# Sparse attention and a Mish layer: three products in other PSUM buffers, and three re-orderings

## The chip, the cores and the metric

The kernel runs on one core of a Trainium2 chip. The metric is the device time of one execution in microseconds (us), as the median of several runs. Five engines work side by side and meet through semaphores: TensorE (PE, with its weight loads shown as PEld), VectorE (DVE), ScalarE (ACT), GpSimd (POOL), and SyncE (SP), which here only issues transfers. Matmul results go to PSUM, which TensorE writes and VectorE and ScalarE read.

## The reference, cut to what matters

Attention over 8 batches of 8 heads, 576 positions, 64 values each. Half of the heads see the 32 positions up to their own ("local", `l`), half those with the same position modulo 32 ("strided", `s`). Then comes a layer of two matrices with a Mish between.

```python
rel = pos[:, None] - pos[None, :]
mask_local = (rel >= 0) & (rel < stride)                 # stride = 32
mask_strided = (rel >= 0) & (pos[None, :] % stride == pos[:, None] % stride)
scores = np.where(masks, scale * q @ k.T, -1e9)
attn = exp(scores - max); attn = attn / sum(attn)
x = (attn @ v), heads side by side                        # 4608 tokens x 512
h = x @ w_in                                              # 512 -> 2048
out = (h * np.tanh(softplus(h))) @ w_out                  # 2048 -> 512
```

## The kernel before

The 4608 tokens are worked off in nine blocks of 512 (`t`), each with a product with `w_in` (`mlp1`), a Mish on ScalarE and a product with `w_out` (`mlp2`). Between the pieces of those products stand the steps of the attention of a later batch: in block `t` that of batch `t + 1`. The first batch stands alone at the head of the program, before the first block.

PSUM has eight banks. Six form three accumulators of two banks (`acc`), two are single buffers that are used in turn (`tile_t`):

```python
def acc(i, name):
    return ps_a.tile([128, 2, 512], F32, tag=f"acc{i}", name=name)

def tile_t(name):
    return ps_t.tile([128, 512], F32, tag="pt", name=name)      # pool with bufs=2
```

Transposes (`t_step_loc0` for q and k, `xt` for the attention's result) and the products with v share the two single buffers. A product with v, `pv`, computes four heads' parts and, in column D, the sum of the weights; VectorE then takes the reciprocal and multiplies, which empties the buffer:

```python
def pv(self, kind, i):
    po = tile_t("po")[:, 0:4 * (D + 1)].rearrange("p (h d) -> p h d", h=4)
    m = WQ if kind == "l" else PN
    self.pv_mm(kind, i, po)
    ...
    nc.vector.reciprocal(rden[0:m, :], po[0:m, :, D])
    nc.vector.tensor_tensor(out=dst..., in0=po[0:m, :, 0:D], in1=rden..., op=ALU.mult)
```

`pv2` does two of them at once in an accumulator (first batch only). `qk(parts, i_acc)` computes scores into an accumulator, from which ScalarE writes the exponentials to SBUF; `mask` multiplies them by a mask on VectorE. The kind "n" is the strided scores of the next batch but with another division into parts.

The steps of batches 2 and 3 (blocks 1 and 2); the list's place i is run after the i-th of 16 pieces of `mlp2`. `x, y, z` are the accumulators. Pieces 0 to 7 sum in z, 8 to 15 in y, and ScalarE copies an accumulator out after its last piece:

```python
Q = lambda i_acc, *parts: (lambda: a.qk(parts, i_acc))
M = lambda kd, i: (lambda: a.mask(kd, i, nc.vector))
V = lambda kd, i: (lambda: a.pv(kd, i))
X = lambda kd, hf: (lambda: a.xt(kd, hf))
...
    [V("s", 4), M(*l0)],                  # 6
    [Q(x, l1), V("s", 5)],                # 7
    [V("s", 6), V("l", 5)],               # 8
    [V("s", 7), M(*l1)],                  # 9
    [V("l", 0), V("l", 1)],               # 10
    [X("s", 0), V("l", 2)],               # 11
    [X("s", 1), V("l", 3)],               # 12
    [V("l", 4), X("l", 0)],               # 13
    [X("l", 1)], [],                      # 14, 15
if z is not None:                         # block 2 only: scores of batch 4
    r[12].append(Q(x, ("n", 0)))
    r[13].append(Q(z, ("n", 1)))
    r[15] += [Q(x, ("n", 2)), M("n", 0), M("n", 1), M("n", 2)]
```

The steps of batch 1 (block 0), where `ts[4]` and `ts[6]` are transposes of k (copied out by VectorE), `ts[5]` and `ts[7]` of q (copied by ScalarE). In this block `mlp2` sums in x and z, and y serves for scores:

```python
    [V("s", 1), M("s", 1), Q(y, ("s", 2))],       # 4
    [V("s", 2), ts[4]],                           # 5
    [V("s", 3), M("s", 2), ts[6], ts[5]],         # 6
    [V("s", 4), ts[7]],                           # 7
    [V("s", 5), Q(y, ("l", 0))],                  # 8
    ...
    [V("l", 3), V("l", 5)],                       # 13
    [V("l", 4), X("l", 0)],                       # 14
    [X("l", 1)],                                  # 15
```

The first batch. `fill` and `fill_acc` are matmuls whose results nobody reads, put where TensorE would otherwise pause:

```python
for i in range(3):
    a.qk([("s", i)], i)                            # scores of s, exponentials
fill(tile_t("fill"), 3)
a.pv2("s", 0, 0)
t_step_loc0(kl0, kTl[:, 0, 32:32 + S], 0, Sc)      # local k, from its transfer lq<-in_k
t_step_loc0(kl0, kTl[:, 1, 32:32 + S], 1, Sc)
a.pv2("s", 2, 1)
a.pv2("s", 4, 2)
fill_acc(0, 2)
t_step_loc0(ql0, qTl[:, 0, :], 0, Sc)              # local q
t_step_loc0(ql0, qTl[:, 1, :], 1, Sc)
a.pv2("s", 6, 0)
for i in range(2):
    a.bias("l", i, i + 1)                          # the mask as a matmul
for i in range(2):
    a.qk([("l", i)], i + 1)
for hp in range(2):
    rows_v_loc01(0, hp, Dv)                        # rows of v, VectorE
...
a.xt("s", 0, Dv)
a.xt("s", 1)
fill_acc(0, 2)
a.pv2("l", 0, 1)
a.bias("l", 2, 0)
a.qk([("l", 2)], 0)
a.pv2("l", 2, 2)
gT, g1 = mlp1(0, accs)                             # accs = (1, 2, 0)
g1.pop(0)()                                        # first large product
```

Of the kernel before, what the change touches and what calls it, by code (L numbers as in the profile page):

```python
# [40 lines left out]
def kernel(ctx, tc, q, k, v, moe_w_in, moe_w_out, out):  # L41
    nc = tc.nc
    B, H, S, D = q.shape
# [29 lines left out]
    qTl = const.tile([128, 2, S], BF16, name="qTl")  # L73
# [16 lines left out]
# [5 lines that stand above are left out]
        return ps_t.tile([128, 512], F32, tag="pt", name=name)  # L95
# [49 lines left out]
    def copy_v_str01(b, eng, j0, j1):  # L145
        cast(
            eng, vs[b % 2][0:PN, :, j0:j1, 0:D],
            vsd[b % 2].rearrange("p (h j d) -> p h j d", h=4, j=CS)[:, :, j0:j1, :],
        )
# [27 lines left out]
    def cast(eng, out_, in_):  # L177
        if eng is nc.scalar:
            nc.scalar.copy(out_, in_)  # L179
        else:  # L180
            eng.tensor_copy(out_, in_)  # L181
# [15 lines left out]
    def str_by_dma(b):  # L197
        for src, dst in ((ks, kTs), (qs, qTs)):
            nc.sync.dma_start_transpose(
                sT(dst, b)[:, 0:16 * SU].rearrange("c (u n) -> c u n", u=16),  # L200
                src[b % 2][0:SU].rearrange("p h x -> p (h x)"),
            )
# [45 lines left out]
    def t_step_loc0(src, dst, hp, eng):  # L248

        tr = tile_t("tr")[:].bitcast(BF16)  # L250
        for j in range(CL):
            for e in range(2):
                nc.tensor.transpose(  # L253
                    tr[64 * e:64 * e + 64, PL * j:PL * j + PL], src[0:PL, 2 * hp + e, j, :],
                    ident[0:PL, 0:PL],
                )
        cast(
            eng, dst.rearrange("c (p j) -> c p j", j=CL),
            tr[:, 0:S].rearrange("c (j p) -> c p j", j=CL),
        )  # L260
# [26 lines left out]
    class Attn:  # L287
# [85 lines left out]
                        start=True, stop=True,  # L373
                    )

        def pv(self, kind, i):
            po = tile_t("po")[:, 0:4 * (D + 1)].rearrange("p (h d) -> p h d", h=4)
            m = WQ if kind == "l" else PN
            self.pv_mm(kind, i, po)
            dst = (x_l if kind == "l" else x_s)[0:m, i, :]  # L380
            rden = small.tile([128, 4], F32, tag="rden", name="rden")
            nc.vector.reciprocal(rden[0:m, :], po[0:m, :, D])  # L382
            nc.vector.tensor_tensor(  # L383
                out=dst.rearrange("p (h d) -> p h d", h=4), in0=po[0:m, :, 0:D],
                in1=rden[0:m, :].unsqueeze(2).to_broadcast([m, 4, D]), op=ALU.mult,
            )
# [95 lines left out]
            [], [], [], [], [], [], [],  # L482
        ]

    def attn_steps(b, x, y, z=None):

        a = Attn(b)
        Q = lambda i_acc, *parts: (lambda: a.qk(parts, i_acc))
# [3 lines that stand above are left out]
        s0, s1, sl2, l0, l1 = ("s", 0), ("s", 1), (("s", 2), ("l", 2)), ("l", 0), ("l", 1)  # L492
        r = [
            [],
            [Q(x, s0), Q(y, s1), M(*s0), M(*s1)],
            [],
            [V("s", 0), V("s", 1)],
            [Q(x, *sl2), Q(y, l0), V("s", 2)],
            [V("s", 3), M("s", 2), M("l", 2)],
            [V("s", 4), M(*l0)],  # L500
            [Q(x, l1), V("s", 5)],
            [V("s", 6), V("l", 5)],
            [V("s", 7), M(*l1)],
            [V("l", 0), V("l", 1)],
            [X("s", 0), V("l", 2)],
            [X("s", 1), V("l", 3)],
            [V("l", 4), X("l", 0)],
            [X("l", 1)], [],
        ]
        if z is not None:  # L510
            r[12].append(Q(x, ("n", 0)))
            r[13].append(Q(z, ("n", 1)))
            r[15] += [Q(x, ("n", 2)), M("n", 0), M("n", 1), M("n", 2)]
        return r


    def attn_steps1(y, ts):

        a = Attn(1)
# [4 lines that stand above are left out]
        return [  # L524
            [lambda: nc.scalar.preload_act_table(AF.Exp)],
            [Q(y, ("s", 0)), lambda: copy_v_str01(1, nc.vector, 0, CS)],
            [M("s", 0), Q(y, ("s", 1))],
            [V("s", 0)],
            [V("s", 1), M("s", 1), Q(y, ("s", 2))],
            [V("s", 2), ts[4]],  # L530
            [V("s", 3), M("s", 2), ts[6], ts[5]],
            [V("s", 4), ts[7]],
            [V("s", 5), Q(y, ("l", 0))],
            [V("s", 6), M("l", 0), Q(y, ("l", 1))],
            [V("s", 7), V("l", 0), M("l", 1), Q(y, ("l", 2))],
            [X("s", 0), V("l", 1), M("l", 2)],
            [X("s", 1), V("l", 2)],
            [V("l", 3), V("l", 5)],
            [V("l", 4), X("l", 0)],
            [X("l", 1)],  # L540
        ]


    def fill(t, n, w=512):

        for _ in range(n):
            nc.tensor.matmul(
                t[:, 0:w], lhsT=kTs[1][:, 512:640], rhs=kTs[1][:, 0:w], start=True, stop=True
            )
# [86 lines left out]
    with tc.manual_schedule():  # L636
        Po, Dv, Sc = nc.gpsimd, nc.vector, nc.scalar
# [4 lines left out]
        kl0, ql0 = [lq0[:, 1536 * i:1536 * i + 1536].rearrange("p (h x) -> p h x", h=4) for i in range(2)]  # L642
# [7 lines left out]
        kl0, ql0 = [x.rearrange("p h (j d) -> p h j d", d=D) for x in (kl0, ql0)]  # L650
# [26 lines left out]
        a = Attn(0)  # L677
# [12 lines left out]
            a.qk([("s", i)], i)  # L690
        fill(tile_t("fill"), 3)
        a.pv2("s", 0, 0)
        t_step_loc0(kl0, kTl[:, 0, 32:32 + S], 0, Sc)
        t_step_loc0(kl0, kTl[:, 1, 32:32 + S], 1, Sc)
        a.pv2("s", 2, 1)
        a.pv2("s", 4, 2)
        fill_acc(0, 2)
        t_step_loc0(ql0, qTl[:, 0, :], 0, Sc)
        t_step_loc0(ql0, qTl[:, 1, :], 1, Sc)
        a.pv2("s", 6, 0)  # L700
        for i in range(2):
            a.bias("l", i, i + 1)
# [44 lines left out]
        for t in range(NBLK):  # L747
            x, y, z = accs
            if t > 0:
                gT, g1 = mlp1(t, accs)  # L750
            at, a1 = [], []
            if t == 0:
                ts = t_steps1()
                at = attn_steps1(y, ts)
                at[1].append(next_loads)
                at[10] += [lambda: str_by_dma(2), lambda: loc_by_dma(2)]
                out_accs, accs = (z, x), (y, z, x)
            else:
                if t <= 2:
                    at = attn_steps(t + 1, x, y, z if t == 2 else None)  # L760
                elif t + 1 < B:
                    a1 = str_steps(t + 1)
                    at = loc_steps(t + 1, x, y)
                if t == 1:
                    at[9].append(lambda: str_by_dma(3))
                if t == 2:
                    Dv.memset(x_s[64:96], 0.0)
                if t + 2 < B:
                    at[9].append(lambda: loc_by_dma(t + 2))
                if 1 < t < B - 3:  # L770
                    at[9].append(lambda: str_by_dma(t + 3))
                out_accs, accs = (z, y), (z, x, y)
            for i, g in enumerate(g1):
                g()
                if i < len(a1):
                    for s in a1[i]:
                        s()
                if t == 0 and i > 7:
                    for n in ((0, 2), (1, 3))[i - 8]:
                        ts[n]()  # L780
            if t > 0 and t + 2 < B:
                cast_qk_loc(t + 2, Po, Po)
                if 1 < t < B - 3:
                    load_qk_str(t + 3)
                if t < 3:
                    cast_v(t + 2, Po, Po)
                else:
                    at[5].append(lambda: cast_v(t + 2, Po, Po))
            if t == 1:
                load_qk_str(4)  # L790
            if t == NBLK - 1:
                mlp2_last(t, gT, (z, y, x))
                break
            for i, g in enumerate(mlp2(t, gT, out_accs, fc_major=(t == 0))):
                g()
                if i < len(at):
                    for s in at[i]:
                        s()
            if t + 3 < B:
                load_qk_loc(t + 3)  # L800
                if t == 1:
                    str_by_dma(4)
                load_v(t + 3)
# [30 lines left out]
```

The softmax here doesn't subtract the row's maximum and nothing guards it: scores larger than these inputs give would overflow.

## Time and profile before

| | |
|---|---|
| Time, median of 3 runs | 306.92 us (305.93 to 307.51) |
| Span of the profiled execution | 305.2 us |
| TensorE busy | 298.5 us, 98% |
| ScalarE, VectorE, GpSimd busy | 59%, 51%, 34% |
| Granted TensorE clock | full in all slices of the page |

How to read it: the span runs from the first instruction to the last. An engine's line names the source line, the operation, output and input, and how often. In brackets stands the idle time before an instruction and what ended it. The chain follows the work back from the last instruction to what released each step, so that it says which engine set the end at each moment. Names with L and a number are lines of the kernel: L366 is the product with v, L382 and L383 its reciprocal and multiply, L253 the transposes of local q and k, L410 and L420 those of the result, L324 the scores, L338 their exponential, L346 the masks on VectorE, L575 `mlp1`, L599 `mlp2`, L606 the copy of its result. Matmuls overlap and their ends are modelled.

### The profile page before, as it was taken

The page shows a single profiled execution, that of the slowest core. Times are in us where ns is not written, and L with a number is a line of the kernel's source. Part 1 is how long each engine was busy: PE and PEld are TensorE (multiplying, and loading weights), DVE is VectorE, ACT ScalarE, POOL GpSimd, SP SyncE. Part 2 cuts the span into 40 slices and gives each one's busy share as a digit, 9 for nine tenths or more (in the row PEclk, how much of TensorE's full clock was granted, in tenths as well). Part 3 has the DMA queues.
Part 4 walks back from the last instruction along what each step waited for, and adds up shares of the span by engine and source line. Part 5 has one row for each costly group of instructions (what it writes and reads, how often), then busy time and mean ns, then how long its engine had stood idle before and what let it go on. Part 6 is the DMA issues. An engine that isn't in the chain of part 4 may idle for free.

```text
span 305.2 us, 6124 instructions
## 1 busy us (share of the span) xinstructions
PE 298.5 (98%) x2552; PEld 160.0 (52%) x2552; DVE 155.8 (51%) x375; ACT 181.3 (59%) x193; POOL 104.1 (34%) x119
## 2 busy tenths in 40 slices
PE   8999999999999999999999999999999999999995
PEld 7664555544554455444579654445444544444444
DVE  4382366202840077489877888788878850000000
ACT  2676625776456764757965786678668746216501
POOL 8662339930470232405940296029500000000000
PEclk9999999999999999999999999999999999999999
DMA  7999999999999999999769995997520120011011
GB/s 138 169 207 193 206 182 140 157 113 257 181 217 124 227 176 193 165 210 176 107 144 178 190 171 144 169 192 121 128 89 0 54 86 0 2 69 69 0 71 69
DMA packets 97552, 41.83 MB, mean 137 GB/s; under 512 B 79605, under 2 KB 91461, under 8 KB 97525
## 3 DMA queue, kind: packets, MB, share of 16 engines
q1 hardware_dynamic: 71708, 28.84, 52.5%
q0 software_dynamic: 25504, 12.31, 32.9%
q8 instruction: 20, 0.33, 0.4%
q10 hardware_dynamic: 312, 0.28, 0.3%
q14 instruction: 8, 0.06, 0.1%
HBM read 36.82 MB, written 9.44 MB: 152 GB/s over the span
## 4 chain that ended last, share of the span: by engine, by line
PE 91%; DVE 3%; DMA 2%; POOL 1%; issue 1%; ACT 1%; ACTq 0%; POOLq 0%
PE psh L575 41%; PE pso L599 35%; PE po L366 5%; PE pso L626 5%; PE ps L324 3%; DMA lq<-in_k_dram 2%; DVE x_l L383 1%; PE tr L253 1%; PE trx L410 1%; DVE x_s L383 1%; PE trx L420 1%; DVE rden L382 0%; ACT Ps L338 0%; POOL qs L110 0%; POOL vs L110 0%
## 5 line engine op out<-in xcount | busy, mean ns | idle before, releaser
L575 PE MATMUL psh<-xT,w_in 128*128 128x512 bf16 (+3 forms) x648 | 130.6, 355 | 0.6 <-DVE rden L396 0.3
L599 PE MATMUL pso<-w_out,gT 128*128 128x512 bf16 x512 | 121.7, 379 | 0.0
L581 ACT ACTIVATE gT<-psh 128x1024 bf16<-128x1024 f32 x72 | 72.4, 1023 | 46.1 <-PE psh L575 46.1
L575 PEld LDWEIGHTS <-w_in 128*128 128x128 bf16 x648 | 60.8, 98 | 55.1 <-issue 0.9
L599 PEld LDWEIGHTS <-gT 128*128 128x128 bf16 x512 | 45.5, 98 | 46.1
L445 DVE STREAM_TRANSPOSE xs_t<-x_s 32x512 bf16<-32x512 bf16 x48 | 33.7, 702 | 0.9
L606 ACT COPY osb<-pso 128x1024 f32<-128x1024 f32 x16 | 17.6, 1100 | 24.8 <-PE pso L599 14.4
L382 DVE RECIPROCAL rden<-po 72x4 f32<-72x4 f32 (+1 forms) x98 | 17.3, 177 | 28.5 <-PE po L366 28.4
L181 POOL CAST kl<-kl 96x768 bf16<-96x768 f32 x10 | 8.4, 870 | 65.5 <-DMA kl<-in_k_dram 65.5
L346 DVE TENSOR_TENSOR Ps<-Ps,consts_sb 72x864 bf16<-72x864 bf16 (+3 forms) x12 | 7.4, 616 | 40.0 <-ACT Ps L338 40.0
L436 DVE STREAM_TRANSPOSE xT<-x_l 32x384 bf16<-32x384 bf16 x48 | 27.3, 569 | 0.7
L181 DVE COPY osb<-pso 128x512 f32<-128x512 f32 (+1 forms) x2 | 1.1, 558 | 51.3 <-PE pso L626 51.3
L383 DVE TENSOR_TENSOR x_s<-po,rden 72x256 bf16<-72x256 f32 x56 | 23.5, 420 | 1.9
L338 ACT ACTIVATE Ps<-ps 72x864 bf16<-72x864 f32 (+3 forms) x21 | 17.4, 860 | 11.1 <-PE ps L324 11.1
L366 PEld LDWEIGHTS <-Ps 72*128 72x128 bf16 x256 | 15.6, 97 | 11.4 <-DVE Ps L346 0.8
L452 ACT COPY xT<-xs_t 128x576 bf16<-128x576 bf16 x8 | 21.4, 2938 | 0.0
L338 ACT ACTIVATE Pl<-ps 128x960 bf16<-128x960 f32 (+1 forms) x20 | 17.2, 877 | 2.6 <-PE ps L324 2.5
L383 DVE TENSOR_TENSOR x_l<-po,rden 96x256 bf16<-96x256 f32 x42 | 17.7, 420 | 1.4
L366 PE MATMUL po<-vs,Ps 72*128 72x65 bf16 (+1 forms) x256 | 18.1, 194 | 0.0
L181 POOL CAST vl<-vl 128x768 bf16<-128x768 f32 (+2 forms) x20 | 15.6, 779 | 6.1 <-DMA vl<-in_v_dram 5.2
L179 ACT COPY xT<-trx 128x576 bf16<-128x576 bf16 x15 | 9.6, 639 | 12.5 <-PE trx L420 9.6
L346 POOL TENSOR_TENSOR Ps<-Ps,consts_sb 72x1008 bf16<-72x1008 bf16 (+1 forms) x9 | 14.5, 1636 | 0.8 <-DVE x_l L383 0.7
(93 smaller groups left out, 242.9 us busy)
## 6 DMA issues: line engine op xcount, KB each, us to landing
out_dram<-osb SPq DMA_DIRECT2D x16, 512.0 KB, 3.9
kl<-in_k_dram SPq DMA_DIRECT2D x5, 576.0 KB, 7.0
ql<-in_q_dram SPq DMA_DIRECT2D x5, 576.0 KB, 10.6
vs<-in_v_dram SPq DMA_DIRECT2D x5, 576.0 KB
vl<-in_v_dram SPq DMA_DIRECT2D x5, 576.0 KB, 9.6
w_out<-in_moe_w_out_dram POOLq DMA_DIRECT2D x4, 512.0 KB, 14.9
ks<-in_k_dram POOLq DMA_DIRECT2D x7, 288.0 KB, 9.8
qs<-in_q_dram POOLq DMA_DIRECT2D x7, 288.0 KB, 10.0
```

Of the source, the lines that this page charges most:

```text
L181: eng.tensor_copy(out_, in_)
L338: nc.scalar.activation(pt[0:n, :, 0:nw], t[0:n, :, o0:o0 + nw], AF.Exp, scale=scale)
L346: meng.tensor_tensor(out=pm, in0=pm, in1=mk[0:n, :].unsqueeze(1).unsqueeze(1).to_broadcast([n, 2, nu, w]), op=ALU.mult,)
L366: nc.tensor.matmul(po[:, h, 0:rhs.shape[-1]], lhsT=pt[0:n, c0:c0 + 128], rhs=rhs, start=True, stop=True,)
L383: nc.vector.tensor_tensor(out=dst.rearrange("p (h d) -> p h d", h=4), in0=po[0:m, :, 0:D], in1=rden[0:m, :].unsqueeze(2).to_broadcast([m, ...
L436: nc.vector.transpose(dst[32 * q:32 * q + 32, :, :, m:m + 32], src[m:m + 32, :, :, q, :])
L445: nc.vector.transpose(xs_t[32 * q:32 * q + 32, :, :, m:m + 32], src[m:m + 32, :, :, q, :])
L452: nc.scalar.copy(xT[:, 2 + c, t0:t0 + S].rearrange("p (n j) -> p j n", j=CS), xs_t[:, :, c, 0:PN])
L575: nc.tensor.matmul(ps[:, u, o:o + n], lhsT=w_in[:, cc, fc * 128:(fc + 1) * 128], rhs=xT[:, cc, a:a + n], start=(cc == 2 and o == 0), stop= ...
L581: nc.scalar.activation(gT[:, 2 * g:2 * g + 2, :], ps[:], AF.Mish)
L599: nc.tensor.matmul(p[:, ot % 2, :], lhsT=gT[:, fc, 128 * ot:128 * ot + 128], rhs=w_out[:, fc, :], start=(fc == 0), stop=(fc == 15),)
L606: nc.scalar.copy(osb[:], p[:])
```

## The change

Six places. One product of batch 1 (`s` 3) moves from a single buffer to accumulator y, and there the mask of part 2 moves behind the two transposes. A second product of batch 1 (`l` 4) moves to y. The product `l` 5 of batches 2 and 3 moves to z. These are meant to leave the two single buffers to the neighbours. The last scores of batch 4, and the masks of the parts before, move one step ahead, so that their exponential is issued ahead of the copy of the last `mlp2` result. In the first batch the second pair of strided products moves ahead of the transposes of local k, to stand where TensorE would wait for k's transfer, and the copy of half of q moves from ScalarE to VectorE.

```diff
-        def pv(self, kind, i):
-            po = tile_t("po")[:, 0:4 * (D + 1)].rearrange("p (h d) -> p h d", h=4)
+        def pv(self, kind, i, i_acc=None):
+            po = tile_t("po") if i_acc is None else acc(i_acc, "po")[:, 0, :]
+            po = po[:, 0:4 * (D + 1)].rearrange("p (h d) -> p h d", h=4)
...
     def attn_steps(b, x, y, z, more):
...
-            [V("s", 6), V("l", 5)],
+            [V("s", 6), lambda: a.pv("l", 5, z)],
...
-        if z is not None:
+        if more:
             r[12].append(Q(x, ("n", 0)))
             r[13].append(Q(z, ("n", 1)))
-            r[15] += [Q(x, ("n", 2)), M("n", 0), M("n", 1), M("n", 2)]
+            r[14] += [Q(x, ("n", 2)), M("n", 0), M("n", 1)]
+            r[15].append(M("n", 2))
...
-            [V("s", 3), M("s", 2), ts[6], ts[5]],
+            [lambda: a.pv("s", 3, y), ts[6], ts[5], M("s", 2)],
...
-            [V("l", 4), X("l", 0)],
+            [lambda: a.pv("l", 4, y), X("l", 0)],
...
         a.pv2("s", 0, 0)
+        a.pv2("s", 2, 1)
         t_step_loc0(kl0, kTl[:, 0, 32:32 + S], 0, Sc)
         t_step_loc0(kl0, kTl[:, 1, 32:32 + S], 1, Sc)
-        a.pv2("s", 2, 1)
         a.pv2("s", 4, 2)
         fill_acc(0, 2)
         t_step_loc0(ql0, qTl[:, 0, :], 0, Sc)
-        t_step_loc0(ql0, qTl[:, 1, :], 1, Sc)
+        t_step_loc0(ql0, qTl[:, 1, :], 1, Dv)
...
-                    at = attn_steps(t + 1, x, y, z if t == 2 else None)
+                    at = attn_steps(t + 1, x, y, z, t == 2)
```

More of the change, by code (lines that the diff above doesn't have):

```diff
@@ L483, in loc_steps, with attn_steps @@
         ]
-    def attn_steps(b, x, y, z=None):
+    def attn_steps(b, x, y, z, more):
         a = Attn(b)
```

## The prediction

> **What bounds the kernel now.** I read the page first: the busy table, then the chain that ended last.
>
> ```profile
> PE 298.5 (98%) x2552; PEld 160.0 (52%) x2552; DVE 155.8 (51%) x375; ACT 181.3 (59%) x193; POOL 104.1 (34%) x119
> ...
> PE 91%; DVE 3%; DMA 2%; POOL 1%; issue 1%; ACT 1%; ACTq 0%; POOLq 0%
> ```
>
> TensorE carries 91% of the chain and nothing in this change removes work from it. So the change can win only what lies between TensorE's instructions: about 9% of 305 us is the outer limit, much of it the start. Next I listed the waits of TensorE and then read the timeline and the chain in order of time at the places that the diff names. A wait's own figure counts from the modelled end of the matmul before it, and matmuls overlap, so I measure holes from start to start, with these lengths from the chain: a 128x512 matmul 0.216 us (0.86 for four), the four products of one `pv` 0.13, twelve 96-row transposes 0.32 (0.63 for 24).
>
> Batch 1, step 6, the chain in order of time:
>
> ```profile
> 43.51 0.19 DVE rden L382
> ...
> 43.72 0.43 DVE x_s L383
> 44.15 0.14 issue
> 44.29 0.45 PE tr L253 x12
> ```
>
> The transposes of q (L253, at 44.29) want the buffer in which the product s3 stood, and wait for VectorE's reciprocal and multiply. The k transposes before them began at 43.40 and hold 0.32, so the hole is 43.72 to 44.29, **0.57 us**.
>
> Batch 1, step 14, TensorE's timeline:
>
> ```profile
> 54.98 0.29 PE L366 MATMUL po<-vl,Pl 128*128 128x65 bf16 x4
> 55.42 0.43 PE L410 MATMUL trx<-consts_sb,x_l 96*128 96x96 bf16 x6 [0.16 <-DVE x_l L383]
> ```
>
> l4 holds 0.13, so the transposes could begin at 55.11. They begin at 55.42: **0.31 us**, for the buffer of l5.
>
> Batch 2, step 8, the whole timeline (the second VectorE line is the one that counts below):
>
> ```profile
> 79.71 1.01 ACT L606 COPY osb<-pso 128x1024 f32<-128x1024 f32 x1 [1.44 <-issue]
> ...
> 80.88 0.28 PE L366 MATMUL po<-vs,Ps 72*128 72x65 bf16 x4
> 80.97 0.42 DVE L383 TENSOR_TENSOR x_s<-po,rden 72x256 bf16<-72x256 f32 x1
> ...
> 81.49 0.29 PE L366 MATMUL po<-vl,Pl 128*128 128x65 bf16 x4 [0.33 <-PE po L366]
> ...
> 82.81 0.18 DVE L382 RECIPROCAL rden<-po 72x4 f32<-72x4 f32 x1 [0.33 <-PE po L366]
> ```
>
> s6 is through at 81.01, l5 starts at 81.49: a hole of 0.48. The wait is named after a TensorE instruction, which had long been done; what ends just before is VectorE's multiply of s5 (81.39), whose buffer l5 takes. In batch 3 the same step shows no hole: s6 at 113.85 and l5 at 113.97.
>
> The end of that stage, where batch 4's last scores stand:
>
> ```profile
> 123.35 1.01 ACT L606 COPY osb<-pso 128x1024 f32<-128x1024 f32 x1 [0.23 <-PE pso L599]
> 123.41 1.04 PE L575 MATMUL psh<-xT,w_in 128*128 128x512 bf16 x4
> 124.26 0.41 ACT L338 ACTIVATE Ps<-ps 72x288 bf16<-72x288 f32 x1
> ...
> 124.71 0.38 PE L575 MATMUL psh<-xT,w_in 128*128 128x512 bf16 x1 [0.26 <-ACT Ps L338]
> ```
>
> The second group of the next product wants the accumulator of those scores; their exponential stands behind the output copy on ScalarE. 123.41 + 0.86 = 124.27, so the hole is **0.44 us**.
>
> The first batch, the chain:
>
> ```profile
> 4.56 7.49 DMA lq<-in_k_dram
> 12.05 0.04 issue
> 12.09 0.70 PE tr L253 x24
> ...
> 13.75 0.45 PE fill L547 x2
> 14.21 0.63 PE tr L253 x24
> ```
>
> TensorE ends s0 and s1 at about 11.5 and idles until local k has landed at 12.05.
>
> **What the Trainium skill says.** "Perfetto Trace Analysis", Identifying the Most-Contended Engine, holds matmul busy time to be a poor measure of how near TensorE is to its limit; the trace agrees, 98% busy with holes of 0.3 to 0.6 us. The same page, Optimization Strategy, has repeated bubbles on the engine that should be full stand for too few buffers; three of the four holes above are that, each ending with the VectorE instruction that frees a buffer. "PSUM — Partial Sum Buffer", PSUM bank collisions raise a hardware error, asks that engines are kept apart by bank, so a product put into accumulator z must await the output copy that reads z: the end at 80.72 is to be checked, not only VectorE. "TensorE: Matmul & The Clock Gate", Step-by-step, has weight loads pulled ahead only where row groups don't conflict; the trace shows something that fits: scores start at 123.24, 0.10 us after the product before has passed (122.28 + 0.86).
>
> **The change, part by part.** No instruction is added or removed.
>
> (1) s3 of batch 1 in accumulator y, with the two transposes ahead of the mask. y was last read by an exponential that ended at 41.51, so s3 doesn't wait. k then takes the buffer of s2 (free at 42.67), q that of the k transposes before (copied by 43.33): no wait. 24 transposes from 43.40 take 0.63, and 0.07 to the next product, as now: 44.10 in place of 44.67, **0.57**. The mask (0.66) moves behind the copy of k (0.74) on VectorE and ends near 45.5, so s4's multiply ends near 46.2; its buffer is next wanted near 46.4. It is close but does not bind. I take 0.55.
>
> (2) l4 of batch 1 in y: the transposes take l3's buffer, free at 54.82. **0.31**. The transposes of the other half start at about 56.25, after l4's multiply (55.94).
>
> (3) l5 in z. For batch 2, z's output copy ends at 80.72, before 81.01, so l5 starts 0.48 earlier. Not all of it stays: VectorE is without a pause until it has multiplied l5 at 82.48, and its chain of s7, mask, l0 and l1 leads to the next product at 85.16, which waits for it. That chain starts at 82.81 after 0.33 of idle; 0.02 of that is needed between instructions. **0.31**. In batch 3: 0, with the copy ending at 113.69 against 113.97.
>
> (4) Batch 4's last scores: their exponential now comes ahead of the output copy (about 123.0 to 123.45), their accumulator is free before 124.27. **0.44**. The output copy slides to about 124.6; its accumulator is wanted by the third group, after 125.1.
>
> (5) The first batch. The exponential for s2 and s3 ends at 11.78 (two take 1.66 from 10.12). s2 and s3 can then run from 11.85 to 12.29 (two such pairs take 0.87, 12.72 to 13.59), add 0.10 to switch, k transposes 12.39 to 13.02, s4 and s5 to 13.46, two fills to 13.89, switch, q transposes at 13.99 in place of 14.13: 0.14 on TensorE, not 0.43, as k has landed meanwhile. Local q landed about 13.6 (issued 5.60, 8.0 to landing), so that doesn't bind. But the half of q now on VectorE (0.74, the size of the kTl copies) is put ahead of the reciprocal of s6, and VectorE is on the path: s6's multiply now ends at 16.35, then come the v rows, a copy of x, and the reciprocal of l0 at 18.08, which releases the first large product at 19.15. With q's copy from about 14.8 to 15.55, s6's multiply would end near 16.4. ScalarE is freed, but TensorE's 0.83 us of bias matmuls cover its copies (end 15.80) already. I take **0.05**.
>
> Sum: 0.55 + 0.31 + 0.31 + 0.44 + 0.05 = 1.66. From 306.92: **305.3 us**. Behind 125 us TensorE runs from product to product (0.86 and 0.13 in turn), so I see nothing that takes the gain back.
>
> **Rivals.** *A new wait on an accumulator.* In batch 3 l5 trails the output copy by only 0.28; for z to be late in both batches would cost about 0.3 each. For it: ScalarE has the copy, exponentials and more in one row. Against: no change ahead of them. That would make it 305.6 to 305.9. *VectorE becomes the bound* in the first batch and in step 7 of batch 1: the first part would lose some 0.2, the second keep only half: 305.8. *Timed by transfers*: if the early part waited for weights, the early gains vanish. Against it, the first large products wait for no transfer in the list of TensorE's waits. *All holes close and VectorE follows*: the first batch gives its 0.3 as well and batch 2 0.41: 304.9.
>
> **Range and chances.** The parts are independent; 0.3 us of uncertainty for the first batch and 0.2 for each of the others make about 0.5. The three runs before spread over 1.6 us, so a median can be off by 0.5 too. Range 304.3 to 306.4. Two per cent is 6.1 us, more than all holes here together: faster 0.01, same 0.98, slower 0.01.
>
> **What would show it.** In the changed trace: q's transposes right behind k's at about 43.7; the transposes after l4 with no wait on VectorE; l5 0.13 after s6 in batch 2; the first group pair of the stage at 123 without a wait for an exponential; the list of TensorE's waits nearly empty; the first large product at 19.1, not 18.8. I would be wrong if l5 is seen waiting for an output copy, if step 7 of batch 1 waits for VectorE, or if the first large product comes later than 19.15.

## The result, and the profile after

The changed kernel takes 304.99 us in the median of 6 runs (304.85 to 305.34), the kernel before 306.55 us in 6 runs (305.93 to 308.07). The ratio is 0.9943, with a 95% interval of 0.9917 to 0.9969. It is faster by about half a per cent, as forecast (305.3).

From the page of the changed kernel, the busy table and the chain that ended last:

```profile
PE 297.8 (98%) x2552; PEld 159.4 (53%) x2552; DVE 155.8 (51%) x376; ACT 180.9 (60%) x192; POOL 103.6 (34%) x119
...
PE 95%; DVE 3%; ACT 1%; issue 0%; ACTq 0%
```

The busy times are as before: TensorE does the same work in a shorter span. Its share of the chain has risen from 91% to 95%, and the transfer of k has left the chain.

From the list of TensorE's waits of the changed kernel (who waited for whom: us in total, times, longest):

```profile
PE fill L549 <- DVE kTs L653: 1.3, 1, 1.3
PE psh L577 <- DVE rden L397: 0.3, 1, 0.3
PE po L366 <- ACT Ps L338: 0.2, 1, 0.2
```

Seven waits have become three, and the last of them is new: in the first batch the product s2 now waits for an exponential.

TensorE's order is fixed, so the span can be cut at its own instructions and each stretch compared. All times in us, from the two profiled executions:

| Stretch, on TensorE | before | after | gain |
|---|---|---|---|
| Start to the first exponential (ScalarE) | 10.12 | 10.02 | 0.10 |
| to the first large product | 9.02 | 8.84 | 0.18 |
| to the first `w_out` product of block 0 | 15.68 | 15.68 | 0 |
| `w_out` products of block 0, with batch 1 | 21.98 | 21.02 | 0.96 |
| `w_out` products of block 1, with batch 2 | 19.16 | 18.67 | 0.49 |
| `w_out` products of block 2, with batch 3 | 19.82 | 19.82 | 0 |
| from there to batch 4's first product with v | 2.16 | 1.73 | 0.43 |

The `w_in` products between take 13.8 in both, and what follows 179.67 in both. The gains add up to 2.17 before rounding, which is what the two spans differ by. Between the medians it is only 1.56: the profiled execution of before, 307.01 us, lies above that kernel's median, and the one of after, 304.85, a little below its own. The experiments tell which of these gains are always there.

The four places in block 0 to 2, in the changed kernel. The chain, batch 1, step 6 (start, length, what):

```profile
43.18 0.63 PE tr L253 x24
43.81 0.97 PE pso L601 x4
```

k's and q's transposes are now one piece of 24. Before, they were two of 12 with a reciprocal and a multiply of VectorE between. TensorE's timeline, batch 1, step 14:

```profile
54.05 0.29 PE L366 MATMUL po<-vl,Pl 128*128 128x65 bf16 x4
54.18 0.42 PE L411 MATMUL trx<-consts_sb,x_l 96*128 96x96 bf16 x6
```

The transposes begin 0.13 after l4, without a wait. The timeline of batch 2, step 8:

```profile
78.46 1.01 ACT L608 COPY osb<-pso 128x1024 f32<-128x1024 f32 x1 [1.44 <-issue]
...
79.63 0.28 PE L366 MATMUL po<-vs,Ps 72*128 72x65 bf16 x4
79.75 0.29 PE L366 MATMUL po<-vl,Pl 128*128 128x65 bf16 x4
```

l5 comes 0.12 after s6; the output copy that empties z ended at 79.47, 0.28 ahead of it. The timeline at the end of block 2:

```profile
121.27 0.41 ACT L338 ACTIVATE Ps<-ps 72x288 bf16<-72x288 f32 x1
121.68 1.89 PE L577 MATMUL psh<-xT,w_in 128*128 128x512 bf16 x8
121.88 1.01 ACT L608 COPY osb<-pso 128x1024 f32<-128x1024 f32 x1 [0.20 <-PE pso L601]
```

The exponential of batch 4's last scores now stands ahead of the output copy, and the first two groups of `mlp1` run as one piece of eight.

### The profile page after: what moved, and what is told of

The parts are those of the page before. It is cut to its first block, busy times and chain, and to the rows that moved or that the text cites. A ratio compares the mean times of both kernels' runs of the same rounds, so it can differ in the third digit from the quotient of the medians.

```text
span 303.1 us, 6121 instructions
## 1 busy us (share of the span) xinstructions
PE 297.8 (98%) x2552; PEld 159.4 (53%) x2552; DVE 155.8 (51%) x376; ACT 180.9 (60%) x192; POOL 103.6 (34%) x119
## 4 chain that ended last, share of the span: by engine, by line
PE 95%; DVE 3%; ACT 1%; issue 0%; ACTq 0%
PE psh L577 41%; PE pso L601 35%; PE po L366 5%; PE pso L628 5%; PE ps L324 3%; PE fill L549 2%; PE tr L253 1%; ACT Ps L338 1%; DVE x_l L384 1%; PE tr L237 1%; PE trx L411 1%; PE ps L297 1%; DVE x_s L384 1%; PE trx L421 1%; DVE rden L383 0%; DVE Pl L346 0%
```

## The experiments

The theory from the traces was that each hole is an affair of its own and closes for good when its cause is taken away. For batch 2 there was a rival. In the kernel before, VectorE's mask of the strided part 2 had taken 1.01 us, while GpSimd was casting k. Timeline of the kernel before:

```profile
78.24 2.10 POOL L181 CAST kl<-kl 96x768 bf16<-96x768 f32 x2 [10.10 <-DMA kl<-in_k_dram]
...
78.37 1.01 DVE L346 TENSOR_TENSOR Ps<-Ps,consts_sb 72x576 bf16<-72x576 bf16 x1
```

In batch 3 the same mask took 0.45, with no cast beside it, and there was no hole either.

### Each part of blocks 0 to 2 left out alone

The medians alone can't tell one part from another: with the exception of s3's, the ratios below have intervals that overlap the changed kernel's 0.9917 to 0.9969. So what a part is worth is read from the stretches, of one profiled execution each.

**l5 back in a single buffer** (batches 2 and 3):

```diff
-            [V("s", 6), lambda: a.pv("l", 5, z)],
+            [V("s", 6), V("l", 5)],
```

> The changed kernel with l5 of batches 2 and 3 back in a single buffer. Theory A (the hole of batch 2 comes from there being two single buffers): l5 waits again 0.4 to 0.5 us after s6 in batch 2, and the time is 0.3 to 0.5 above the changed kernel, 305.3 to 305.5. Theory B (the hole came because the mask of the strided part 2 took 1.01 us instead of 0.45 in that execution, beside GpSimd's cast of k, and made VectorE late): no wait where that mask takes 0.45, in batch 3 never, and a time within 0.15 of the changed kernel's 305.0.

Measured: 305.39 us, ratio to the kernel before 0.9955 (0.9937 to 0.9973). In the profiled execution l5 didn't wait in either batch; the mask of part 2 took 0.45 in both. The timeline of batch 2:

```profile
79.67 0.28 PE L366 MATMUL po<-vs,Ps 72*128 72x65 bf16 x4
79.79 0.30 PE L366 MATMUL po<-vl,Pl 128*128 128x65 bf16 x4
```

So the hole isn't made by the number of buffers alone, as theory A had it. The stretches were still about 0.28 longer each than in the changed kernel (18.95 and 20.10), and the median is what theory A expected. But the loss is elsewhere: in batch 2 the mask of the local part 1 took 0.92 in place of 0.65, beside GpSimd's cast of q, and in batch 3 a mask of part 0 took 0.88 in place of 0.60. It isn't the buffer's either: with l5 in z, the run with batch 4's scores put back (below) has stretches of 18.97 and 20.07, with 0.94 and 0.86 for the same two masks.

**s3 back in a single buffer, with its mask ahead:**

```diff
-            [lambda: a.pv("s", 3, y), ts[6], ts[5], M("s", 2)],
+            [V("s", 3), M("s", 2), ts[6], ts[5]],
```

> The changed kernel with s3 of batch 1 back in a single buffer and its mask back ahead of the transposes. Sum of holes: q's transposes wait again for s3's multiply, 0.57 to 0.64 us between k's transposes and the next product, time 305.6. Rival (VectorE is behind anyway and takes the gain back later in block 0): under 0.3, time 305.0 to 305.3.

Measured: 305.83 us, ratio 0.998 (0.997 to 0.999). Block 0's stretch is 21.81, 0.79 above the changed kernel's. The hole is back, as TensorE's list of waits has it:

```profile
PE tr L253 <- DVE x_s L384: 0.4, 1, 0.4
```

From k's transposes to q's it is 0.89 against 0.28, which is 0.61 of the 0.79; the rest came a step later, behind a mask that took 0.92 beside GpSimd's copy of rows of v.

**l4 back in a single buffer:**

```diff
-            [lambda: a.pv("l", 4, y), X("l", 0)],
+            [V("l", 4), X("l", 0)],
```

> The changed kernel with l4 of batch 1 back in a single buffer. Sum of holes: 0.31 us ahead of the transposes after l4, time 305.3. Rival (the next block waits for ScalarE's output copy, so the start of the product after it doesn't move): no difference, 305.0.

Measured: 305.34 us, ratio 0.9952 (0.9928 to 0.9976); block 0's stretch 21.35, 0.33 above the changed kernel's. The hole stands at the same place, and the next block starts later by as much.

**Batch 4's last scores back in step 15:**

```diff
-            r[14] += [Q(x, ("n", 2)), M("n", 0), M("n", 1)]
-            r[15].append(M("n", 2))
+            r[15] += [Q(x, ("n", 2)), M("n", 0), M("n", 1), M("n", 2)]
```

> The changed kernel with batch 4's last scores and masks back in step 15. Sum of holes: 0.44 us ahead of the second group of the next product, which waits for the exponential, time 305.4. Rival (the third group or the activation behind it takes the gain back): under 0.2, 305.0 to 305.2.

Measured: 305.40 us, ratio 0.9961 (0.9948 to 0.9975). The way to batch 4's first product is 2.16 again, as before the change, and TensorE's list has the wait back:

```profile
PE psh L576 <- ACT Ps L338: 0.3, 1, 0.3
```

**s3 in y, but the mask ahead of the transposes:**

```diff
-            [lambda: a.pv("s", 3, y), ts[6], ts[5], M("s", 2)],
+            [lambda: a.pv("s", 3, y), M("s", 2), ts[6], ts[5]],
```

> The changed kernel with s3 in accumulator y but its mask ahead of the transposes again. If the buffer alone closes the hole: q's transposes follow k's at once; the mask (0.45 to 0.66) then stands ahead of VectorE's copy of k, whose buffer s4 wants, so s4 would wait some 0.4 to 0.6: time 305.4. If the order of the mask doesn't matter: 305.0.

Measured: 305.18 us, ratio 0.9966 (0.9955 to 0.9978); block 0's stretch 21.64, 0.62 above the changed kernel's. In this execution the whole gain of the buffer is gone. The timeline shows where to:

```profile
43.59 0.42 PE L253 MATMUL tr<-consts_sb,ql 96*64 96x96 bf16 x12
...
43.97 0.96 DVE L346 TENSOR_TENSOR Ps<-Ps,consts_sb 72x576 bf16<-72x576 bf16 x1
...
44.85 0.74 DVE L181 COPY kTl<-tr 128x576 bf16<-128x576 bf16 x1
...
45.65 0.45 PE L253 MATMUL tr<-consts_sb,ql 96*64 96x96 bf16 x12 [0.55 <-DVE kTl L181]
```

q's first transposes (43.59) come at once, but VectorE does the mask ahead of its copy of k, so the buffer of k comes free late and the next transposes wait for it. The hole has moved one step on. But the mask was a slow one, 0.96 in place of 0.45, beside GpSimd's copy of rows of v. With 0.45 the copy of k would end 0.51 sooner, and about 0.1 of the 0.62 would be left (an estimate). The medians lie between: on the same chip the kernel that differs from the changed one in the copy of q alone ("the new order alone", below) took 304.94, 0.24 less than this one, which is within the spread of either's runs. So the order can matter, and how much depends on the mask.

### The first batch

**Both edits of the first batch undone:**

```diff
-        a.pv2("s", 2, 1)
         t_step_loc0(kl0, kTl[:, 0, 32:32 + S], 0, Sc)
         t_step_loc0(kl0, kTl[:, 1, 32:32 + S], 1, Sc)
+        a.pv2("s", 2, 1)
...
-        t_step_loc0(ql0, qTl[:, 1, :], 1, Dv)
+        t_step_loc0(ql0, qTl[:, 1, :], 1, Sc)
```

> The changed kernel with both edits of the first batch undone: s2 and s3 behind k's transposes, both halves of q copied by ScalarE. From the two traces the head gained 0.19 (first exponential to first large product 9.03 before, 8.84 after): 305.2. The prediction's 0.05 would give 305.05, and 9.03 to 8.98 for the stretch.

**The new order alone** (q's copy back on ScalarE), and **the split of q alone** (the order back), each by one half of that diff:

> The changed kernel with q's second half back on ScalarE, the early s2 and s3 kept. If the order alone makes the gain (TensorE's bias matmuls cover ScalarE's copies): stretch from the first exponential to the first large product 8.84 or below, as VectorE is also spared 0.76 us: 305.0 or 304.9. If the split of q is needed: the scores of l wait for ScalarE's second copy, stretch near 9.0, 305.15.

> The changed kernel with the order of before, q's second half on VectorE. If VectorE's copy stands in the path (as the prediction had it): stretch 9.1 to 9.2, the multiply of s6 some 0.1 to 0.2 later than before's 16.35, time 305.3. If it stands in a gap of VectorE: 9.03, 305.2.

Measured, all on one chip: 304.51 us with both undone (ratio 0.995, 0.9937 to 0.9963), 304.94 with the new order alone (0.9962, 0.9949 to 0.9975), 304.84 with the split alone (0.9956, 0.9944 to 0.9968). The stretch from the first exponential to the first large product was 8.52, 8.84 and 8.52. All expectations for the old order missed: it was the faster one. That for the new order alone held. The chain of the kernel with both edits undone:

```profile
11.03 0.11 PE po L366
11.53 0.63 PE tr L253 x24
...
18.52 1.02 PE psh L577 x4
```

and that of the changed kernel:

```profile
10.02 1.67 ACT Ps L338 x2
11.69 0.04 issue
...
12.31 0.63 PE tr L253 x24
...
18.86 1.02 PE psh L577 x4
```

In the first, k had landed at 11.06, while TensorE was still at s0 and s1, so k's transposes follow at once and fill the time until the second exponential is ready. In the changed kernel s2 and s3 come first and must wait for that exponential until 11.69. So each order waits for one thing, the old one for k, the new one for the exponential. Told from the first exponential, k landed between 0.87 and 2.01 in the 14 profiled executions of this study. The old order took:

| k landed after | 0.87 | 1.06 | 1.83 | 1.92 | 2.01 |
|---|---|---|---|---|---|
| stretch, old order | 8.52 | 8.52 | 8.93 | 9.02 | 9.12 |

(The 1.83 and 2.01 are of the two kernels made from the one before, below; 1.92 is the profile before.) It rises as k is later, one for one. The new order took 8.84 in seven of eight executions and 8.93 in one, with k landing anywhere from 1.07 to 1.75. The lines cross at about 1.74. Whether VectorE copies half of q changes nothing in either order: 8.84 with it and without it, 8.52 with it and without it. The medians agree only in part: against 304.94 of the new order, the two kernels with the old one took 304.51 and 304.84 in 5 runs each, so what the old order is worth on average stays open.

### A late VectorE, made and avoided

Does the batch-2 hole come from a mask that runs beside GpSimd? GpSimd casts when k and q have arrived, so the meeting is a matter of chance. Two kernels take the chance away. **The kernel before with its casts held back** until the last mask of blocks 1 and 2 (and two further places that leave out the earlier casts):

```diff
+        def late_casts(b):
+            scr = small.tile([128, 4], BF16, tag="scr", name="scr")
+            Po.tensor_copy(scr[0:32, :], P_l[1][0:32, 0, 0:4])
+            cast_qk_loc(b, Po, Po)
+            cast_v(b, Po, Po)
...
+                if t in (1, 2):
+                    at[9].append(lambda: late_casts(t + 2))
```

> The kernel before, with GpSimd's casts of k, q and v in blocks 1 and 2 held back until the last mask of the block (a four-element copy that reads its result). No mask then runs beside a cast. Theory B (late VectorE makes the hole): the mask of the strided part 2 takes 0.45 us in both blocks, l5 follows s6 within 0.15 us though it still stands in a single buffer, and the stretch of block 1 from its first w_out product to the next block is 18.67 us, as in the changed kernel, in place of 19.16. Theory A (two single buffers are too few): the hole of 0.5 stays and the stretch is 19.1.

Measured: block 1's stretch 18.67, block 2's 19.82. l5 stands in a single buffer and doesn't wait. The timeline of batch 2:

```profile
77.97 0.45 DVE L346 TENSOR_TENSOR Ps<-Ps,consts_sb 72x576 bf16<-72x576 bf16 x1
...
80.48 0.29 PE L366 MATMUL po<-vs,Ps 72*128 72x65 bf16 x4
80.60 0.29 PE L366 MATMUL po<-vl,Pl 128*128 128x65 bf16 x4
```

The time was 306.31 us, ratio 0.9997 (0.9982 to 1.0012): over many executions the held-back casts don't pay by themselves.

**Then the same with two copies by GpSimd set beside the mask**, in the kernel before and in the changed one. These copies are extra work:

```diff
+        def beside_mask():
+            scr = small.tile([128, 4], BF16, tag="scr", name="scr")
+            Po.tensor_copy(scr[0:32, :], x_s[0:32, 2, 0:4])
+            for _ in range(2):
+                Po.tensor_copy(junk[0:96, :], w_in[0:96, 0, 0:1024])
...
                 if t in (1, 2):
+                    at[4].append(beside_mask)
                     at[9].append(lambda: late_casts(t + 2))
```

> The kernel before with the casts held back and two copies of 96x1024 bf16 by GpSimd set beside the mask of the strided part 2 in blocks 1 and 2 (started by the product s2; extra work, its result is not used). Theory B: that mask takes about 1.0 in both blocks, l5 waits 0.5 after s6, and block 1's stretch is 19.1 or more, block 2's 20.3. Theory A: as without the copies, 0.5 in block 1 and none in block 2 (19.16 and 19.82).

> The changed kernel with the same held-back casts and the same two extra copies. Theory B, with accumulator z as a cover against a late VectorE: the mask takes about 1.0, l5 still follows s6 at once, the stretches are 18.67 and 19.82. If z covers only the wait at l5 and the lateness comes out further on: 18.9 to 19.0 and 20.1.

Timeline of the kernel before with the copies, batch 2:

```profile
77.37 2.51 POOL L752 COPY junk<-w_in 96x1024 bf16<-96x1024 bf16 x2
...
78.09 0.62 DVE L347 TENSOR_TENSOR Ps<-Ps,consts_sb 72x576 bf16<-72x576 bf16 x1
...
79.45 0.94 DVE L347 TENSOR_TENSOR Pl<-Pl,consts_sb 128x960 bf16<-128x960 bf16 x1
...
80.60 0.29 PE L367 MATMUL po<-vs,Ps 72*128 72x65 bf16 x4
...
81.04 0.29 PE L367 MATMUL po<-vl,Pl 128*128 128x65 bf16 x4 [0.16 <-PE po L367]
```

Timeline of the changed kernel with the copies, batch 2:

```profile
76.99 0.62 DVE L347 TENSOR_TENSOR Ps<-Ps,consts_sb 72x576 bf16<-72x576 bf16 x1
...
78.36 0.94 DVE L347 TENSOR_TENSOR Pl<-Pl,consts_sb 128x960 bf16<-128x960 bf16 x1
79.50 0.29 PE L367 MATMUL po<-vs,Ps 72*128 72x65 bf16 x4
79.62 0.29 PE L367 MATMUL po<-vl,Pl 128*128 128x65 bf16 x4
```

The masks are equally slow in both (0.62 and 0.94, against 0.45 and 0.64 undisturbed). With a single buffer l5 starts 0.44 after s6, which is a hole of 0.31; with z it follows at once. Against 18.67 and 19.82 the stretches are 18.98 and 20.25 in the kernel before, 18.67 and 19.87 in the changed one. Times: 306.99 us (ratio 1.0009, 0.9994 to 1.0024) and 305.03 us (0.9952, 0.9938 to 0.9966). The first is 0.68 above the same kernel without the copies, and the two stretches lost 0.74. The mask came to 0.62, not 1.0 as expected, as GpSimd's copies fell otherwise against it than the cast had, but together with the next mask it made VectorE late enough, in both batches. So both theories had a part: a slow mask makes VectorE late, and only with the single buffer does that reach TensorE at l5.

The case of the kernel before also came about by itself with l5 in z: in batch 3 of the kernel with both edits of the first batch undone, the mask of part 2 ran beside a cast of k. VectorE's and TensorE's timelines:

```profile
109.25 1.02 DVE L346 TENSOR_TENSOR Ps<-Ps,consts_sb 72x576 bf16<-72x576 bf16 x1
...
111.76 0.29 PE L366 MATMUL po<-vs,Ps 72*128 72x65 bf16 x4
111.88 0.29 PE L366 MATMUL po<-vl,Pl 128*128 128x65 bf16 x4
```

l5 follows at once, and VectorE starts the mask of the local part 1 as long after the block's first `w_out` product as in the changed kernel (12.25): z left nothing of the hole. The block's stretch was 20.08 all the same, about 0.25 above the changed kernel's. This mask took 0.90 beside a cast of q, and the transposes that wait for VectorE's multiplies behind it came late by that much. So z covers a late VectorE at l5, not at the places after it.

Holding the casts back can move the meeting elsewhere. In the changed kernel with the copies, the last mask of batch 4 (72x288) took 2.02 in place of 0.29, beside the cast of v, and batch 4's first product came 0.22 later than in the changed kernel (1.95 in place of 1.73).

### A further version

**The changed kernel with the first batch as before but without the two fills ahead of q's transposes, l1 of batches 2 and 3 also in z, and the casts held back:**

```diff
-            [V("l", 0), V("l", 1)],
+            [V("l", 0), lambda: a.pv("l", 1, z)],
...
         a.pv2("s", 4, 2)
-        fill_acc(0, 2)
```

> The changed kernel with the first batch as before (which was 8.52 us from the first exponential to the first large product where k had landed, against 8.84), without the two fills ahead of q's transposes, with the product l1 of batches 2 and 3 also in z, and with the casts held back. Expected: l2 follows the transposes without its wait of 0.28 in both blocks, stretches of 18.39 and 19.54; no slow mask; first batch 8.1 to 8.5. Time 303.9 to 304.2. Rival for the fills: VectorE's row of copies sets the first large product, 8.5; rival for the held-back casts: batch 3's transposing transfers come too late for its scores, over 305.

Measured: 305.37 us in the median, ratio 0.9953 (0.9934 to 0.9972), with runs from 303.53, the lowest of the study, to 309.13. Eight of the 20 runs had a granted clock of 0.994 and took 305.69 to 309.13, while the other twelve, at 0.998 to 1.0, have a median of 304.2, as expected; why the lower clock came so often here, against 2 of 49 runs of the kernel before on the same chip, isn't shown.

In the profiled execution (306.44 us) block 1 was 18.36, 0.30 below the changed kernel, for l1 in z. The first batch was 8.51, so leaving out the fills gave nothing over the 8.52 with them, as the rival had it. Block 2 was 21.54; its timeline shows why:

```profile
118.80 0.40 PE L324 MATMUL ps<-qTs,kTs 64*128 64x72 bf16 x14 [1.96 <-DMA qTs<-qs]
```

Batch 4's scores waited 1.96 us for the transfer that transposes its q. In this execution that transfer was issued at 114.89, in the changed kernel at 109.62, behind the transfers on SyncE's queue that wait for the casts. That the held-back casts alone are to blame isn't shown, as the kernel before with the same casts (issued at 110.60) didn't wait. Nor does the wait look like the rule: it cost this block 1.72, and this execution lies 2.3 above the median of the twelve. Over all runs, the lowest median is that of the changed kernel with the first batch left as before, 304.51 us in 5 runs.

## Why the prediction was right, and where it wasn't

The time of 305.3 and the range held, and so did the way to it: read TensorE's holes from start to start, see for each what follows on it. The sum of 1.66 lies between the 1.56 of the medians and the 2.17 of the two profiled executions. But two of its five terms weren't the fixed gains that it took them for. Three held wherever they were looked at: 1.30 was predicted for (1), (2) and (4) together, and 1.39 measured between the traces. The other 0.36 rested on what happened in one execution, and that the sum came so near is partly luck.

- **(1) s3 in y.** Predicted 0.55. Between the two traces q's transposes come 0.61 sooner after k's (0.28 in place of 0.89) and the next product 0.64; undoing it cost 0.61 there and 0.79 with what followed. The step that was off by a little is the 0.07 to the next product: 24 transposes and the change to the product take 0.63 together. That the mask behind the copy of k would be "close" was too careful: s4's multiply ended at 45.57, and the next product in its buffer started at 46.09. With the mask ahead, 0.62 was lost in one execution, behind a slow mask, and 0.24 in the medians.
- **(2) l4 in y.** Predicted 0.31; 0.32 between the traces (block 0's 0.96 less the 0.64 above), 0.33 by undoing it.
- **(3) l5 in z.** Predicted 0.31 for batch 2 and 0 for batch 3; 0.49 and 0 between the traces, and no hole in either batch where l5 was put back. The step that failed is the reading of the wait: the prediction named the right VectorE multiply but took its lateness for granted, as part of the schedule. With masks of their usual length there is no hole, whichever buffer l5 has. The prediction also took it for one of the repeated gaps that stand for too few buffers; "Perfetto Trace Analysis", Optimization Strategy, of the Trainium skill says only that they can mean this, and this one didn't repeat in batch 3. "SBUF — State Buffer", Who interferes with whom, of the Trainium skill has it that a VectorE instruction with two SBUF inputs contends with a GpSimd instruction that reads SBUF, and that one waits for the other to end. These masks are such instructions, and the traces agree: 0.45 became 0.62 to 1.02 and 0.65 up to 1.10 beside GpSimd's casts or copies. VectorE's multiply of s5 ended late in that one execution, and the 0.5 was that execution's. What z gives is a cover: 0.31 and 0.38 in the two batches where the disturbance was made (18.98 less 18.67, 20.25 less 19.87), nothing where there is none. The size may have been off too: the prediction kept 0.31 of the 0.48, as VectorE had no pause to catch up in, but with l5 in z and a mask of 1.02 (batch 3, above) it had caught up by the mask of the local part 1.
- **(4) Batch 4's last scores.** Predicted 0.44, measured 0.43, both ways.
- **(5) The first batch.** Predicted 0.05; 0.18 between the traces; and 0.32 lost where k has landed in time. Two steps failed. That VectorE with q's copy "is on the path" was wrong. Already in the kernel before, the reciprocal of l0 waited for TensorE (VectorE's timeline), and so it does in the changed kernel (chain):

```profile
18.08 0.20 DVE L396 RECIPROCAL rden<-po 96x8 f32<-96x8 f32 x1 [0.19 <-PE po L366]
```

```profile
17.50 0.27 PE po L366 x8
17.77 0.02 issue
17.79 0.21 DVE rden L397
```

VectorE's copy of x had ended at 17.66, and the split of q made no difference to the stretch in any run. The first large product came at 18.86 (0.10 of that is an earlier start), so the sign "19.1, not 18.8" missed. And "local k has landed at 12.05" was one execution's arrival: it is the term to which the gain hangs, and with an earlier k the sign turns.

The rivals: no product l5 waited for an output copy that reads z, in any trace of a kernel that has l5 there. Nothing was given back later; the 179.67 after batch 4's start are the same in both.

Left open: how often, over many executions, k is late and a mask is slow. In the profiles of the ten kernels without held-back casts the mask of part 2 was slow in 2 of the 20 stretches of blocks 1 and 2; counting slow masks of all parts, 6 of the 20 lost 0.25 to 0.49.

## What to carry to other kernels

A hole in one trace has a cause that may itself be an accident of that execution: before giving it a fixed worth, look at the same step in another batch or another run, and at how long the releasing instruction and those ahead of it usually take. A spare buffer at such a place is worth having as a cover against a late engine even where it brings nothing on a good day; and when a buffer is added, look at the order of the engine that frees its neighbours too, or the wait can move one step on. An order that fills the wait for a transfer should be judged over a range of arrivals, not by one.

## What the runs showed of the hardware

That a VectorE multiply of two SBUF operands stretches beside GpSimd I had not expected to matter here: 72x576 went from 0.45 to 1.01 us beside a cast of 96x768, 128x960 from 0.65 to 0.94. It goes both ways: the second of the two casts in the kernel before took 1.31 where an undisturbed one takes 0.82. VectorE's multiplies out of PSUM (72x256) kept their 0.42 in the same stretches.

The stretching is a wait for an end. All 13 stretched 72x576 masks of the 14 profiles ended 0.30 to 0.31 after the GpSimd instruction that was under way when they began, and the stretched 128x960 masks 0.51 to 0.52 after it. So the loss depends on how much of that instruction is left, up to the 2.02 of the 72x288 mask beside the cast of v, which took 1.89. Not every overlap does it: a 128x960 mask that began 0.30 after a cast of k took its usual 0.64, and the cast took 1.63.
